# A planner that counts TensorE's instructions: 64-token recurrence blocks and an MLP on one core

## The chip, the core and the metric

The kernel runs on one core of a Trainium2 chip. Five engines share the core's SBUF: TensorE (matrix products, into PSUM), VectorE, ScalarE, GpSimd, and SyncE, which here only issues DMAs. The metric is device time in microseconds (us), median over several executions. One further execution was recorded by the hardware profiler; the page and the trace come from that one.

In the profile the engines are PE (TensorE's products), PEld (TensorE's weight loads, which overlap PE), DVE (VectorE), ACT (ScalarE), POOL (GpSimd) and SP (SyncE).

## What is computed

The first block is a linear recurrence (RWKV-6) over 768 tokens for 4 batches and 8 heads of 48 channels. Its output, with the heads side by side, is a row of 384 channels a token, which goes through a layer norm and a two-layer MLP with a residual.

```python
for t in range(S):
    kt, vt, rt, wt = (k[:, :, t], v[:, :, t], r[:, :, t], w[:, :, t])
    cur = np.einsum('bhd,bhe->bhde', u[None] * kt, vt)
    y[:, :, t] = np.einsum('bhd,bhde->bhe', rt, state + cur)
    state = wt[:, :, :, None] * state + np.einsum('bhd,bhe->bhde', kt, vt)
x = y.transpose(0, 2, 1, 3).reshape(B, S, H * D)
xn = (x - mean(x)) / np.sqrt(var(x) + 1e-06) * g_ln
out = x + np.maximum(xn @ w_ch1, 0.0) @ w_ch2        # 384 -> 1536 -> 384
```

## The kernel before

**Tiling.** The work is cut into 8 rounds: 4 batches by 2 halves of 384 tokens. A round has two units of 4 heads. Inside a round the recurrence is worked in blocks of 64 tokens by six levels of doubling. At level `lev`, `quads` multiplies `r` by `k` for the pairs of half blocks of that level, `keep` copies the wanted part of the result from PSUM into the matrix `A` (VectorE, under a mask), and `grow` multiplies `k` and then `r` in place by the decays of half a block (VectorE). So a round is a chain of quads, grow k, grow r, quads, and so on, six times over. Then `states` forms the sums that go from block to block, a scan on VectorE carries them, and `outputs` adds the parts up. `normalize`, `turn_x` and `mlp` follow; in the last three rounds the second layer of the MLP is done by `thirds`.

**Quarter products.** `quads`, `states` and `outputs` use a quarter of TensorE's array at a time, and four products in different quarters run beside each other. The planner calls them `tiled`. The products are very short. A float32 product takes two passes, and a pass is a weight load and a product, so a call of `quads` for both units is 192 instructions, `states` 96 a unit, and `outputs` up to 192 a unit. The other products (transposes, the MLP) use the whole array.

**Who sets the order.** No engine's order is written out by hand. Every step is handed to `Plan.add` (line 78) with its engine or engines, a planned cost in us, what it reads and writes, the tiles that it needs and a priority (40 times the round, plus a stage; the MLP's products are 200 later, so they fill). `Plan.order` (line 104) then plays the program forward: it keeps for each engine the time from which it is free, finds in `start_of` (line 123) when each ready step could start, and takes for the earliest engine the step with the smallest priority among those that could start within `WAIT` of the first. The steps are issued in the order of these planned starts, and each engine runs its own in that order, through the wrapper `InOrder` (line 32), whose calls all come from line 40. That is why nearly every row of the profile has line 40.

Constants of the planner (line 63): `HOP` 0.1 us from the end of a step to the start of one on another engine; `STAY` 12, a penalty on a change between quarter and whole products; `DRAIN` (line 64), 0.1 and 0.12 us for such a change.

**VectorE and GpSimd.** Small steps (`totals`, `own`, `own_term`, `halve`, `halve2`) may go to either. A step with `port=True`, and any that may go to GpSimd, is planned so that it doesn't run beside another such step on the other engine. On GpSimd it is planned beside a VectorE step without that mark, if there is one. In the program nothing holds it there: it starts as soon as its own inputs are ready.

**Filling.** In the first 90 planned us `idle` (line 1407) puts products of zeros into gaps over 0.4 us on TensorE.

Of the kernel before, what the change touches and what calls it, by code (L numbers as in the profile page):

```python
# [29 lines left out]


class InOrder:
    def __init__(self, tc, engine):
        self.tc, self.engine = tc, engine

    def __getattr__(self, name):
        f = getattr(self.engine, name)
        if not callable(f):
            return f
        return lambda *args, **kw: self.tc.keep_in_program_order(f(*args, **kw))  # L40


class Op:
    def __init__(self, i, costs, fn, pri, lat, size, port, tiled):
        self.i, self.costs, self.fn, self.pri = i, costs, fn, pri
        self.lat, self.size, self.port, self.tiled = lat, size, port, tiled
        self.need, self.next, self.new, self.uses = set(), [], [], set()
        self.ready, self.end, self.eng = 0.0, None, None


class Plan:
# [10 lines left out]

    HOP, PATIENCE, STAY = 0.1, 15.0, 12
    DRAIN = {True: 0.1, False: 0.12}
# [12 lines left out]

    def add(self, eng, cost, fn, r=(), w=(), new=(), pri=0, lat=0.0, size=0, port=False, tiled=False):
        costs = {eng: cost} if isinstance(eng, str) else dict(zip(eng, cost))
        op = Op(len(self.ops), costs, fn, pri, lat, size, port or "POOL" in costs, tiled)  # L80
        self.ops.append(op)
        for tag, name in new:
            self.tile_tag[name] = tag
            op.new.append((tag, name))
            self.queue[tag].append(op.i)
            self.maker[name] = op.i
        for key in list(r) + list(w):
            if key in self.writer:
                op.need.add(self.writer[key])
            name = key[0] if isinstance(key, tuple) else key  # L90
            op.uses.add(name)
        for tag, name in new:
            op.uses.add(name)
        for key in w:
            op.need.update(self.readers.pop(key, ()))
            self.writer[key] = op.i
        for key in r:
            self.readers.setdefault(key, set()).add(op.i)
        op.uses = {n for n in op.uses if n in self.tile_tag}
        op.need.update(self.maker.get(n, op.i) for n in op.uses)  # L100
        op.need.discard(op.i)
        return op

    def order(self, busy, idle=None, until=0.0):
        ops = self.ops
# [11 lines left out]
        for op in ops:  # L117
            if not left[op.i]:
                for e in op.costs:
                    ready[e].append(op)  # L120
        dma, todo, out, tiled = 0.0, len(ops), [], False

        def start_of(op, e):
# [15 lines left out]
            return t  # L139

        while todo:
            best = None
            for e, waiting in ready.items():
                at = [(t, op) for op in waiting if (t := start_of(op, e)) is not None]
                if not at:
                    continue
                first = min(t for t, _ in at)
                t, op = min(
                    ((t, op) for t, op in at if t <= first + self.WAIT[e]),
                    key=lambda x: (  # L150
                        x[1].pri + self.STAY * (e == "PE" and x[1].tiled != tiled), x[1].i
                    ),
                )
                if best is None or t < best[0]:
                    best = t, op, e
            assert best
            t, op, e = best
            if idle and e == "PE" and t < until and t - free["PE"] > 0.4 and self.homes[idle[0]]:
                n = int((t - free["PE"]) / (idle[1] * (2 if t < 5.0 else 1)))
                home = min(self.homes[idle[0]])  # L160
                if n and home[0] <= free["PE"]:
                    out.append((free["PE"], lambda n=n, home=home: idle[2](n, home[1])))
                    self.homes[idle[0]].remove(home)
                    self.homes[idle[0]].append((t, home[1]))
            if e == "PE" and op.tiled != tiled:
                tiled = op.tiled
                t += self.DRAIN[tiled]
            for x in op.costs:
                ready[x].remove(op)
            op.eng, op.start, cost = e, t, op.costs[e]  # L170
            free[e] = t + cost
# [16 lines left out]
            for j in op.next:  # L188
                nxt = ops[j]
                hop = self.HOP if set(nxt.costs) != {e} else 0.0  # L190
                nxt.ready = max(nxt.ready, op.end + hop)
                left[j] -= 1
                if not left[j]:
                    for x in nxt.costs:
                        ready[x].append(nxt)
            fn = op.fn
            out.append((t, fn if len(op.costs) == 1 else lambda fn=fn, e=e: fn(e)))
            todo -= 1
        return [fn for _, fn in out]


# [3 lines left out]
def kernel(  # L205
# [179 lines left out]
    def turn(nm, q, pr, stage):  # L385
# [20 lines left out]
        def keep(e="ACT"):  # L406
# [7 lines left out]
        plan.add(  # L414
            "PE", 0.66 if rows else 0.33, go, r=[key, (name, uu, pr)], w=[ps],
            new=[("b", ps)] + new, pri=at(rnd, stage), lat=0.17,
# [105 lines left out]
    def quads(rnd, lev, us=both_units):  # L522
        n, name = 1 << lev, f"a{rnd}_{lev}"

        def go():
# [21 lines left out]
            w=[(name, uu) for uu in us], new=[("a", name)] if us[0] == 0 else [],  # L547
            pri=at(rnd, 7 + 2 * lev), lat=0.17, tiled=True,
        )
# [82 lines left out]
    def turn_k(q, pr):  # L632
# [17 lines left out]
        key = (name, uu, pr)  # L650
        plan.add("PE", 0.33, go, r=[key], w=[ps], new=[("b", ps)], pri=at(rnd, 20), lat=0.17)
        plan.add("ACT", 0.45, back, r=[ps], w=[key], pri=at(rnd, 20) + EVICT / 2)
# [40 lines left out]
    def states(q):  # L693
# [19 lines left out]
        def scan():  # L713
# [19 lines left out]
            "PE", 0.55, go, r=parts_of(f"k{rnd}", [uu]) + [f"v{q}"], w=[kv_],  # L733
            new=[("a", kv_), ("s", s_)], pri=at(rnd, 22), lat=0.17, tiled=True,
        )
# [21 lines left out]
    def outputs(q, before):  # L757
# [4 lines left out]
        def go():  # L762
# [37 lines left out]
            w=[y_], new=[("a", y_)] + ([("x", x_)] if uu == 0 else []), pri=at(rnd, 24), lat=0.17,  # L800
            tiled=True,
        )
# [77 lines left out]
    def turn_x(rnd, kc):  # L880
# [15 lines left out]
        if rnd >= THREE:  # L896
# [4 lines left out]
        plan.add(  # L901
            "PE", 0.33, go, r=[f"xn{rnd}_{i}" for i in range(TT)], w=[ps], new=new,
            pri=pri, lat=0.17,
# [209 lines left out]
    def thirds(rnd, f):  # L1113
# [34 lines left out]
        for i in range(TT):  # L1148
# [42 lines left out]
            if first:  # L1191
                need += [(f"x{NR - 1}", uu, j) for uu in both_units for j in range(2)]
            plan.add(
                "PE", 0.525, both, r=need, w=keys,
                new=[("a" if i < 2 else "b", n) for n in names] if first else [],
# [7 lines left out]
    def mlp(rnd):  # L1203
# [3 lines left out]
        for f in range(FC):  # L1207
# [3 lines left out]
            if rnd < THREE:  # L1211
# [8 lines left out]
                def relu(f=f, ps=ps, h_=h_):  # L1220
                    ACT.activation(out=tile_("h", h_, [P, RN]), in_=tiles[ps], func=AF.Relu)

                plan.add(
                    "PE", 1.95, go,
                    r=[(f"w1_{g}", kc) for kc in range(KC)] + [f"xf{rnd}_{kc}" for kc in range(KC)],
# [38 lines left out]
            def relu(h_=h_):  # L1264
                ACT.activation(out=tiles[h_], in_=tiles[h_], func=AF.Relu)

            plan.add(
                "PE", 0.53, go_d, r=[d_] + [x_keys(rnd, kc)[2] for kc in range(KC)], w=[ps_d, ps_d + "t"],
                new=[("b", ps_d), (tag, h_)], pri=pri,
# [3 lines left out]
            plan.add(  # L1273
                "PE", 1.12, go,
                r=[(f"wl{g}", kc) for kc in range(KC)] + [(f"wh{g}", kc) for kc in range(KC)]
# [11 lines left out]
        for i in range(TT):  # L1287
            o = f"o{rnd}_{i}"
            for f in range(0, FC, KC):
                def go(f=f, i=i, o=o):  # L1290
# [8 lines left out]
                plan.add(  # L1299
                    "PE", 1.95, go,  # L1300
                    r=[f"h{rnd}_{f_}" for f_ in range(f, f + KC)] + [f"ffn2_{f_}" for f_ in range(f, f + KC)],
# [147 lines left out]
```

## Time and profile before

The times of three executions are 549.24 (the median), 553.76 and 548.67 us. The profiled execution took 550.61 us, of which its span, from the first to the last instruction, is 548.9 us.

| what | us | note |
|---|---|---|
| span of the profiled execution | 548.9 | 20355 instructions |
| the profiled execution itself | 550.61 | 1.7 us around the span |
| mean granted clock of TensorE | 0.993 | as a share of full speed |
| the chain's share of TensorE | 76% | of VectorE 14%, DMA 4%, "issue" 3% |
| quads' products (`a<-r,k`) | 70.0 busy | 4608 passes, 212 ns each, overlapping |
| MLP, second layer (`o<-ffn,h`) | 123.7 busy | 360 passes |
| grow on k and r (`k<-k,tot`, `r<-r,tot`) | 44.4 and 44.0 busy | 45 each, on VectorE |
| GpSimd in all | 84.7 busy | 111 instructions |

"Busy" is the time in which an engine had an instruction of that group under way. The chain is followed back from the last instruction, at each step to what released it; its shares say where time would have to go for the end to move. "issue" means that the engine waited for nothing that the profile shows.

### The profile page before, as it was taken

Reading aid. Unit: us, or ns where it says so; the run is one execution under the profiler, and the core shown is the slowest. Engines: PE = TensorE matmul, PEld = TensorE weight load, DVE = VectorE, ACT = ScalarE, POOL = GpSimd, SP = SyncE. Lnnn points to the kernel's source line nnn. Section 1 sums busy time; section 2 is a strip of 40 time slices with the busy share of each in tenths; the row PEclk is TensorE's granted clock in tenths of the full one; section 3 lists DMA queues with packets and bytes.
Section 4 is the critical chain, followed back from the end, with each engine's and each line's share of the span. In section 5 each row is a group of like instructions: output and inputs, shape, how many; then the busy total and the mean of one; then the engine's idle time right before and its main releaser. Section 6 shows DMA issues by size and latency. Waiting matters only on the chain.

```text
span 548.9 us, 20355 instructions
## 1 busy us (share of the span) xinstructions
PE 523.8 (95%) x8928; PEld 429.5 (78%) x8928; DVE 409.5 (75%) x806; ACT 266.4 (49%) x579; POOL 84.7 (15%) x111
## 2 busy tenths in 40 slices
PE   8999999999999989899999999999999999999995
PEld 7776676666887667688876789758866999999994
DVE  5797999878988969889897697714854856756554
ACT  4787987642654442364640683605830433333321
POOL 7032004701212152103410020000300000000000
PEclk9998999999999999999999999999999999999999
DMA  9974854457453627437540244104201311312201
GB/s 276 260 197 99 247 135 74 99 139 197 121 113 59 165 45 139 85 82 145 120 102 22 54 107 103 36 16 110 68 16 43 116 59 59 100 59 86 73 2 43
DMA packets 118840, 55.83 MB, mean 102 GB/s; under 512 B 86880, under 2 KB 115680, under 8 KB 118752
## 3 DMA queue, kind: packets, MB, share of 16 engines
q1 hardware_dynamic: 117168, 53.65, 38.9%
q8 instruction: 70, 1.15, 0.9%
q10 hardware_dynamic: 1584, 0.88, 0.6%
q14 instruction: 18, 0.15, 0.1%
HBM read 45.05 MB, written 7.10 MB: 95 GB/s over the span
## 4 chain that ended last, share of the span: by engine, by line
PE 76%; DVE 14%; DMA 4%; issue 3%; SPq 2%; ACT 1%; POOL 0%; DVEq 0%; POOLq 0%; ACTq 0%
PE a L40 21%; PE o L40 17%; PE h_ps L40 17%; PE hd_ps L40 7%; DVE k L40 3%; DVE r L40 3%; PE w_ps L40 2%; PE idle L40 2%; PE k_ps L40 2%; PE o_2P L40 2%; SPq L40 2%; PE kn_ps L40 2%; DVE x L40 1%; PE xT_ps L40 1%; PE r_ps L40 1%
## 5 line engine op out<-in xcount | busy, mean ns | idle before, releaser
L40 PE MATMUL o<-ffn,h 128*128 128x384 f32 x360 | 123.7, 489 | 0.0
L40 PEld LDWEIGHTS o<-ffn,h 128*128 128x128 f32 x360 | 65.7, 190 | 37.9
L40 PEld LDWEIGHTS a<-r,k 48*63 48x63 f32 (+5 forms) x4608 | 63.8, 126 | 27.5 <-DVE r L40 11.1
L40 PE MATMUL a<-r,k 48*63 48x32 f32 (+5 forms) x4608 | 70.0, 212 | 10.3 <-DVE r L40 5.4
L40 ACT COPY h<-hd_ps 128x384 f32<-128x384 f32 x84 | 40.0, 479 | 74.5 <-PE hd_ps L40 72.9
L40 DVE SCALAR_TENSOR_TENSOR h<-h_ps,h 128x384 f32<-128x384 f32 x84 | 46.2, 553 | 34.2 <-PE h_ps L40 33.4
L40 PE MATMUL h_ps<-xhl,wl 128*128 128x384 f32 x252 | 61.0, 350 | 0.3
L40 PE MATMUL h_ps<-xhl,wh 128*128 128x384 f32 x252 | 58.0, 338 | 0.0
L40 PE MATMUL hd_ps<-xd,d 128*128 128x384 f32 x252 | 56.8, 351 | 0.6 <-DVE h L40 0.5
L40 DVE TENSOR_TENSOR k<-k,tot 112x768 f32<-112x768 f32 (+1 forms) x45 | 44.4, 987 | 14.1 <-PE a L40 13.9
L40 PEld LDWEIGHTS h_ps<-xhl,wl 128*128 128x128 f32 x252 | 43.7, 188 | 3.5 <-ACT h L40 1.1
L40 PEld LDWEIGHTS hd_ps<-xd,d 128*128 128x128 f32 x252 | 44.1, 190 | 2.2 <-DVE h L40 1.2
L40 PEld LDWEIGHTS h_ps<-xhl,wh 128*128 128x128 f32 x252 | 45.5, 188 | 0.0
L40 DVE TENSOR_TENSOR r<-r,tot 112x768 f32<-112x768 f32 (+1 forms) x45 | 44.0, 977 | 0.0
L40 DVE COPY_PREDICATED A<-mask,a 128x768 f32<-128x768 int8 x32 | 38.5, 1203 | 3.5 <-PE a L40 3.5
L40 POOL TENSOR_TENSOR rk<-nat,nat 128x576 f32<-128x576 f32 x11 | 18.5, 1680 | 143.1 <-DVE own L40 68.0
L40 ACT ACTIVATE hH<-h 128x384 fp32r<-128x384 f32 x36 | 18.8, 525 | 41.1 <-DVE h L40 41.1
L40 ACT ACTIVATE h<-h 128x384 f32<-128x384 f32 x48 | 25.1, 526 | 27.9 <-DVE h L40 27.6
L40 DVE SCALAR_TENSOR_TENSOR hL<-h,hH 128x384 fp32r<-128x384 f32 x36 | 20.0, 555 | 14.3 <-ACT hH L40 14.1
L40 ACT COPY A<-a 32x384 f32<-32x384 f32 x32 | 14.9, 467 | 30.0 <-PE a L40 27.4
L40 ACT COPY w<-w_ps 112x384 f32<-112x384 f32 x32 | 14.4, 482 | 27.5 <-PE w_ps L40 26.9
L40 PE MATMUL a<-w2d,hD 128*128 128x384 f32 x72 | 25.4, 353 | 0.8 <-DVE hD L40 0.7
(118 smaller groups left out, 1020.6 us busy)
## 6 DMA issues: line engine op xcount, KB each, us to landing
d<-w1d SPq DMA_DIRECT2D x84, 192.0 KB, 2.7
raw<-in_moe_w_ch_dram SPq DMA_DIRECT2D x24, 384.0 KB, 4.0
v<-in_v_dram SPq DMA_DIRECT2D x48, 96.0 KB, 3.2
out_dram<-x SPq DMA_DIRECT2D x24, 192.0 KB, 2.0
nat<-in_w_dram SPq DMA_DIRECT2D x36, 96.0 KB, 3.0
nat<-in_k_dram SPq DMA_DIRECT2D x36, 96.0 KB, 2.9
nat<-in_r_dram SPq DMA_DIRECT2D x36, 96.0 KB, 2.8
vx<-v SPq DMA_DIRECT2D x32, 72.0 KB, 2.9
```

Source lines behind the costliest of these rows:

```text
L40: return lambda *args, **kw: self.tc.keep_in_program_order(f(*args, **kw))
```

## The change

1. Every TensorE step gets a `count`, the number of its instructions: 6 for three transposes of one pass, 12 where there are two passes, 96 for each unit of `quads` and `states`, 192 (176 in the first round) for `outputs`. `order` keeps a running `count`, starting at 50, and the time `ahead` at which the next piece of 256 instructions is there. `fetches` goes over the borders between pieces that a step would cross: it adds the wait until that piece is there, and sets the next one 4.3 us later. The wait is added to the step's planned cost.
2. When a step is chosen on TensorE, a step that would wait for a piece by more than 0.2 us gets 300 added to its priority (`switching`), which puts it behind the fillers.
3. From 60 planned us on, a quarter product counts as ready 0.3 us after what it needs has ended, where it was 0.1 us.
4. A `port` step on GpSimd gets extra dependencies. If the VectorE step planned last (`beside`) is still running in the plan, the GpSimd step waits in the program for what that step needs and for the VectorE step before it (`before`); if it isn't, it waits for `beside` itself. What the GpSimd step needs anyway, and steps of GpSimd, are left out. `InOrder` adds these to the first instruction of the step as data dependencies.

```diff
 class InOrder:
+    waits, last = [], None
...
-        return lambda *args, **kw: self.tc.keep_in_program_order(f(*args, **kw))
+        def call(*args, **kw):
+            ins = self.tc.keep_in_program_order(f(*args, **kw))
+            for other in InOrder.waits:
+                self.tc.add_manual_dep(ins.ins, other.name, AFTER, reason="port")
+            InOrder.waits, InOrder.last = [], ins.ins
+            return ins
...
-    HOP, PATIENCE, STAY = 0.1, 15.0, 12
+    HOP, MARGIN, FILLED, PATIENCE, STAY = 0.1, 0.3, 60.0, 15.0, 12
+    BEFORE, PIECE, FETCH, CROWD = 50, 256, 4.3, 300
...
+        count, ahead = self.BEFORE, 0.0
+        beside = before = None
...
+        def fetches(t, op):
+            waits, after = 0.0, ahead
+            for at in range(-count % self.PIECE, op.count, self.PIECE):
+                now = t + waits + op.costs["PE"] * at / op.count
+                waits += max(after - now, 0.0)
+                after = max(now, after) + self.FETCH
+            return waits, after
+
+        def switching(t, op):
+            drain = self.DRAIN[op.tiled] * (op.tiled != tiled)
+            waits = fetches(t + drain, op)[0] > 2 * self.DRAIN[True]
+            return self.STAY * (op.tiled != tiled) + self.CROWD * waits
...
-                    key=lambda x: (
-                        x[1].pri + self.STAY * (e == "PE" and x[1].tiled != tiled), x[1].i
-                    ),
+                    key=lambda x: (x[1].pri + (switching(*x) if e == "PE" else 0), x[1].i),
...
+                    count += 4 * -(-n // 3)
...
+            fetched = 0.0
+            if e == "PE":
+                fetched, ahead = fetches(t, op)
+                count += op.count
...
-            op.eng, op.start, cost = e, t, op.costs[e]
+            op.eng, op.start, cost = e, t, op.costs[e] + fetched
...
-                hop = self.HOP if set(nxt.costs) != {e} else 0.0
+                hop = 0.0 if set(nxt.costs) == {e} else self.HOP
+                if nxt.tiled and self.FILLED < op.end:
+                    hop = self.MARGIN
...
+            if e == "DVE":
+                beside, before = op, beside
+            if e == "POOL" and op.port:
+                others = set(beside.need) if beside and beside.end > t + 0.05 else set()
+                others |= {x.i for x in (before if others else beside,) if x}
+                others -= op.need
+                others = [ops[i] for i in sorted(others) if ops[i].eng not in (None, "POOL")]
+            else:
+                others = ()
+            out.append((t, lambda fn=fn, op=op, others=others: self.run(fn, op, others)))
...
-            "PE", 0.7 * len(us) * (C - n + 6) / (C + 6), go,
...
-            pri=at(rnd, 7 + 2 * lev), lat=0.17, tiled=True,
+            pri=at(rnd, 7 + 2 * lev), lat=0.17, tiled=True, count=96 * len(us),
```

## The prediction

> **What bounds the kernel now.** I read the page's busy row and chain first, then the waits of TensorE, its timeline at those waits, the fetch queue, and a table of windows.
>
> ```profile
> PE 523.8 (95%) x8928; PEld 429.5 (78%) x8928; DVE 409.5 (75%) x806; ACT 266.4 (49%) x579; POOL 84.7 (15%) x111
> ...
> q8 instruction: 70, 1.15, 0.9%
> ...
> PE 76%; DVE 14%; DMA 4%; issue 3%; SPq 2%; ACT 1%; POOL 0%; DVEq 0%; POOLq 0%; ACTq 0%
> ```
>
> TensorE is busy in all but 25.1 us of 548.9, and the chain runs through it. Its work doesn't change, so only idle time, fillers and a lower clock can be won. The waits of TensorE (us in total, times, longest):
>
> ```profile
> PE a L40 <- issue: 8.0, 7, 1.5
> PE a L40 <- DVE r L40: 5.4, 7, 1.2
> ```
>
> Timeline rows of such a wait, idle time and releaser in brackets:
>
> ```profile
> 226.58 2.30 PE L40 MATMUL a<-r,k 48*32 48x32 f32 x175
> 230.42 0.43 PE L40 MATMUL a<-r,k 48*63 48x32 f32 x17 [1.54 <-issue]
> ```
>
> 192 passes of two levels of quads, back to back, stop after 175 for a reason that no semaphore explains. Counting TensorE's records in order (weight loads, products, and waits that are instructions of their own), the seven "issue" stalls come before records 705, 1985, 4289, 5057, 6593, 8385 and 9665: each 193 more than a multiple of 256. Queue 8 carried 70 packets, 1.15 MB, 16 KB or 256 instructions each. The stalled records follow the landing of the last packet by 1.25 to 1.56 us. So TensorE waits for instructions: **8.0 us**.
>
> The clock, in the windows (the figure after POOL's count is the granted clock):
>
> ```profile
> 228.00:230.00 2.00, 0.88 (x63) 0.77 (x56) 1.90 (x3) 1.52 (x4) 0.00 (x0) 1.00 0.31 107
> ...
> 232.00:234.00 2.00, 2.00 (x10) 1.64 (x8) 0.00 (x0) 1.32 (x3) 0.49 (x2) 0.50 0.00 0
> ```
>
> It is at a half in two spells of 3.4 us, at 46.6 and 230.9 us, right after the 1.27 and 1.54 us stalls: 1.7 us lost in each.
>
> The rest of the idle time, from gaps over 0.4 us: eleven gaps between 35 and 393 us that end on VectorE or ScalarE, 0.57 + 0.84 + 0.43 + 0.46 + 0.83 + 1.23 + 0.86 + 0.77 + 0.78 + 0.74 + 0.50 = **8.0 us**; the start, 1.2; the last sums and stores, 4.6. The start and end stay.
>
> [...]
>
> ```profile
> L40 DVE TENSOR_TENSOR r<-r,tot x45: 544/951/2170, 18.9 to 350.2; 112x768 f32<-112x768 f32 x35, 112x384 f32<-112x384 f32 x10
> ...
> L40 DVE TENSOR_TENSOR vo<-v,own x7: 743/759/2391, 44.3 to 319.6; 128x576 f32<-128x576 f32 x7
> ```
>
> (minimum, median, longest in ns.) [...]
>
> **Part 1: counting and holding back.** Quads for both units, 192 instructions, take about 1.40 us (the chain's pieces of 96 passes: mostly 1.2 to 1.6), so 256 of them run in 1.87 us. A piece needs some 3.0 us: the next fetch mostly began 0.7 to 1.6 us after a border, the packet takes 0.9, and the first instruction follows 1.3 later. I laid the built kernels' instruction orders out in pieces from record 193, and priced a piece's passes at 0.0146 us for quads and outputs (1.40/96), 0.0115 for states, 0.324 for `o` (1.94/6), 0.176 for `hd_ps` and its like (1.06/6), 0.11 for transposes (1.33/12), and the planner's 0.11 for a change of kind. Pieces under 3.2 us:
> - before, nine: 2.71, 2.36, 2.99, 1.87, 2.84, 1.87, 1.87, 2.46, 2.26. Five of them stalled (1.27, 1.14, 0.75, 1.04, 1.54); the other two stalls (1.19, 1.06) followed a fetch that began over 3 us late.
> - after, eight: 2.71, 3.06, 1.87, 1.87, 1.87, 2.43, 2.08, 1.87.
>
> So short pieces do **not** go away. The reason is in the count: it leaves out the waits that are instructions of their own (116 in the trace) and starts at 50, where the trace has the first border at 193, so 63. Laid out by the planner's own count the changed order has only four pieces under 3.3 us; by the record the borders come 13 to some 100 instructions earlier. Price after: five pieces near 1.87 to 2.08 at 1.0 (of such pieces before: 1.14, 1.04, 1.54, and 2.26 with none; mean 0.93) is 5.0, and 0.7 for the rest: 5.7. Saved **2.3 us**; ends 0 and 6.
>
> **Part 2: the margin, and the order that follows.** What TensorE has to do between the end of one level's quads and the next level's, against grow k and grow r (0.95 each) and two hops: before, 8 of the 35 such places in rounds 1 to 7 have under 3.0 us (2.16 to 2.91); after, 4 (2.22 to 2.91), and the median goes from about 4 to 7 us. Gaps of 8.0 us halve: **4.0 us** saved; ends 0 and 7. What this costs: the later levels come up to 9 us of TensorE work later, and the MLP behind them is lacking as cover later on. The end isn't exposed: from 400 us TensorE is dense, and the pieces of the built orders from the 64th on hold the same work within 2%.
>
> **Part 3: fillers.** Five passes fewer, two products of 384 and one of 256: 2 x 0.65 + 0.43 = 1.7 us. They stand in idle time; I take half, **0.9**; ends 0 and 1.7.
>
> **Part 4: the ties.** 61 operations of GpSimd on two inputs are left of 75; 53 of them wait for VectorE (26 before) and 42 for TensorE (4 before), that is for the quarter product that the VectorE step beside them needs. Behind a waiting one stand GpSimd's later steps; what waits for those is VectorE's `own` sums, `grow` (by `tot`), the scans (by `decay`) and `x<-a,vo`. Before, no wait of VectorE ends on GpSimd, and GpSimd has 0% of the chain, so a small delay is free. Moved to VectorE, by the built orders: `tot` and `decay` 2 x 0.95 + 2 x 0.56 + 4 x 0.36 + 2 x 0.26 + 2 x 0.21 + 0.18 = 5.6; `rk` 4 x 0.75 = 3.0; `vo` 2 x 0.76 = 1.5; `w1diff` less `w1rest` 0; five `w2t` back to GpSimd, -2.8: **+7.3 us of VectorE**, most of it between 60 and 340 us, where it is busy 84% (201.64 of 240 from 100 to 340). Against it stands stretching[...]: grow k 35 x (1.111 - 0.951) = 5.6, grow r 5.3 with the short form, `vo` 2.8, `w2t` 1.6, `w1diff` 1.2: 16.5 us, of which the ties may take half. VectorE's 14% of the chain against 75% busy puts about a fifth of either on the path: -1.6 and +1.4. Net 0; ends -3 and +6, since a consumer on VectorE held by GpSimd is not shown before.
>
> **Part 5: the clock.** Two spells, 1.7 us each. The first piece pair (1.87, 1.87, near 50 us) is no better than before; I leave both. Ends -3.4 and +3.4.
>
> Sum: -2.3 - 4.0 - 0.9 + 0 = -7.2 us. Against the profiled execution's 550.6 (548.9 and 1.7 around it) that is 543.4. It stands 1.4 above the median of 549.24, so in terms of the median **542 us**.
>
> **Rivals.**
> - *Nothing moves.* The miscounted borders only place the stalls elsewhere (8.0 again), and what the margin saves is lost where cover is missing later. For it: eight short pieces against nine. Against it: fewer places with thin cover. 549, within 3.
> - *GpSimd comes late* (slower). The 42 operations that now wait for a quarter product start with their neighbour on VectorE and end 1.2 to 1.7 us (`vo`, `rk` on GpSimd) later; if every third holds an in-order VectorE step by one grow's length, 14 x 0.95 = 13 us, and the gain elsewhere is 4, the time is 558. It decides from when VectorE's waits for GpSimd pass some 7 us and TensorE's gaps before `a` grow with them. For it: VectorE is full in places (19.65 of 20 from 140 to 160 us). Against it: VectorE idles 139 us, and GpSimd has fewer chains of `tot`.
> - *The count works after all*: 8.0 us of stalls, one spell of low clock (1.7) and 5 of the gaps go: 534. For it: by its own count the order is nearly clean, and a fetch that begins early covers a piece of 2.3. Against it: the layout above.
>
> **How the numbers follow.** A measurement of this kernel can tell about 1% (5.5 us) from no change. Forecast (up to 546, the full count with 0.12 among it) 0.54; nothing moves (546 to 552) 0.28; GpSimd late (over 552) 0.18. Of the first some 0.50 lies below 543.7 (1% under 549.24) and 0.04 above; of the last 0.02 lies under 554.7. So faster 0.50, within 1% 0.34, slower 0.16. The range of 8 in 10 leaves out 0.06 below 534 (half of the full count's) and 0.14 above 554 (0.04 of the last case is under it): 534 to 554.
>
> **What would show it.** Right: "issue" before `a` on TensorE at 5 to 6 us, still at records 193 past a multiple of 256; gaps that end on `r` of VectorE halved; the longest grow under 1.5 us; no wait of VectorE on GpSimd over 3 us. Wrong: "issue" near 0 (the count holds) or over 8; VectorE waiting for GpSimd; new gaps before 400 us that end on VectorE's `own`, `tot` or `x`; more spells at half clock.

## The result, and the profile after

The change moved the time by almost nothing. Over 20 executions each, the changed kernel takes 548.79 us (median; 545.65 to 555.92) and the kernel before, beside it on the same chip, 550.55. The ratio is **0.9978, with a 95% interval of 0.9957 to 0.9999**: 0.2% faster, where 542 us and a clear gain had been forecast.

The profiled execution took 552.50 us (span 550.8), 3.7 above its own median; that of before, 550.61, lies at the median of its twenty (550.55). Ratios leave disturbed executions out and medians don't, so the two needn't agree, and sizes below come from the ratios; of the run *tr* only two of 13 executions were left, and not the profiled one, so its ratio is shown and not used.

Four lines of the page of the changed kernel: busy time, granted clock by fortieths of the span, the fetch queue, the chain.

```profile
PE 526.4 (96%) x8922; PEld 431.7 (78%) x8922; DVE 403.8 (73%) x820; ACT 266.1 (48%) x579; POOL 66.4 (12%) x97
...
PEclk9988999999999999979999999999999999999999
...
q8 instruction: 70, 1.15, 0.9%
...
PE 83%; DVE 7%; DMA 3%; ACT 3%; issue 2%; SPq 1%; DVEq 0%; ACTq 0%
```

VectorE's share of the chain has halved, from 14% to 7%. TensorE has 2.6 us more of busy time for six passes fewer, and the clock row suggests why: it dips in the third and fourth slice and in the 18th. The spells at half clock are 3.4 us at 36.2, 6.8 at 49.8 and 6.8 at 237.6, where before had 3.4 at 46.6 and 3.4 at 230.9. The mean clock of this execution is 0.982 (0.993 before).

TensorE's waits (us in total, times, longest):

```profile
PE a L49 <- issue: 7.4, 8, 1.8
PE kn_ps L49 <- DVE k L49: 2.1, 1, 2.1
...
PE h_ps L49 <- issue: 1.0, 1, 1.0
...
PE a L49 <- DVE r L49: 0.9, 1, 0.9
...
PE hd_ps L49 <- issue: 0.5, 1, 0.5
```

The three "issue" rows make 8.9 us in ten stalls (8.0 in seven before). Each of the ten still stands at a record 193 past a multiple of 256: 961, 1217, 1473, 1985, 2241, 4545, 5313, 7105, 8641 and 13761. The longest in the timeline:

```profile
211.27 1.41 PE L49 MATMUL a<-r,k 48*60 48x32 f32 x89
214.47 0.31 PE L49 MATMUL a<-r,k 48*60 48x32 f32 x7 [1.79 <-issue]
```

Quads stop after 89 of their 96 passes, and the last 7 come 1.79 us later with no semaphore between them. A short piece isn't the only way to such a stall. Four of the ten (records 1985, 4545, 7105 and 8641, 5.2 us) end a piece that TensorE got through in 1.8 to 2.6 us. Five (961, 1217, 1473, 2241 and 13761, 3.2 us) end a piece that lasted 4.2 to 5.9 us; there the packet with the next piece began only 3.0 to 5.1 us after the border before. The tenth (5313, 0.5 us) had a packet that took 1.9 us. Four of those five lie before 54 us; why fetches begin so late there no run shows.

The rest of the idle time did shrink: gaps over 0.25 us between 30 and 420 us that aren't at a border fell from 8.0 us (11) to 6.2 (7). The row of grow r (duration in ns: least, median, longest):

```profile
L49 DVE TENSOR_TENSOR r<-r,tot x45: 545/951/958, 18.7 to 362.8; 112x768 f32<-112x768 f32 x35, 112x384 f32<-112x384 f32 x10
```

The median is as before; the longest is 958 where it was 2170. No grow r is stretched any more. Whether the ties or the new order did that, *no_ties* below tells.

So the things that the change was to improve went different ways: VectorE's part did improve, the fetch stalls didn't, and the clock got worse. That asks which part did which.

### The profile page after: what moved, and what is told of

It is laid out like the page before. It is cut to its first block, busy times and chain, and to the rows that moved or that the text cites. A ratio compares the mean times of both kernels' runs of the same rounds, so it can differ in the third digit from the quotient of the medians.

```text
span 550.8 us, 20398 instructions
## 1 busy us (share of the span) xinstructions
PE 526.4 (96%) x8922; PEld 431.7 (78%) x8922; DVE 403.8 (73%) x820; ACT 266.1 (48%) x579; POOL 66.4 (12%) x97
## 4 chain that ended last, share of the span: by engine, by line
PE 83%; DVE 7%; DMA 3%; ACT 3%; issue 2%; SPq 1%; DVEq 0%; ACTq 0%
PE a L49 23%; PE o L49 21%; PE h_ps L49 19%; PE hd_ps L49 7%; PE r_ps L49 3%; PE w_ps L49 2%; PE k_ps L49 2%; PE o_2P L49 2%; PE kn_ps L49 2%; DVE x L49 2%; PE xT_ps L49 1%; DMA raw<-in_moe_w_ch_dram 1%; PE idle L49 1%; PE o_2D L49 1%; ACT held L49 1%
## 5 line engine op out<-in xcount | busy, mean ns | idle before, releaser
L49 PEld LDWEIGHTS a<-r,k 48*32 48x32 f32 (+5 forms) x4608 | 64.3, 127 | 22.7 <-issue 12.3
L49 DVE SCALAR_TENSOR_TENSOR h<-h_ps,h 128x384 f32<-128x384 f32 x84 | 46.6, 556 | 44.7 <-PE h_ps L49 42.9
L49 PE MATMUL a<-r,k 48*32 48x32 f32 (+5 forms) x4608 | 70.2, 213 | 7.0 <-issue 5.9
L49 DVE TENSOR_TENSOR k<-k,tot 112x768 f32<-112x768 f32 (+1 forms) x45 | 39.3, 872 | 22.3 <-PE a L49 21.9
L49 DVE TENSOR_TENSOR r<-r,tot 112x768 f32<-112x768 f32 (+1 forms) x45 | 38.8, 863 | 0.0
L49 PEld LDWEIGHTS a<-v,A 64*64 64x64 f32 x384 | 22.1, 138 | 5.2 <-issue 3.6
```

The costliest lines, as they stand in the source:

```text
L49: ins = self.tc.keep_in_program_order(f(*args, **kw))
```

## The experiments

"Border" is the idle time of TensorE in stops over 0.25 us at records 193 past a multiple of 256, "other" that of its other gaps over 0.25 us that end between 30 and 420 us, both from the one profiled execution, in us; "clock" is the mean granted clock over all executions of that kernel.

| run | what it has | ratio to before, 95% | median us | clock | border | other |
|---|---|---|---|---|---|---|
| (before) | | | 550.5 | 0.993 | 8.0 | 8.0 |
| (the change) | ties, margin, count | 0.9978 [0.9957, 0.9999] | 548.8 | 0.985 | 8.9 | 6.2 |
| same | nothing | 0.9985 [0.9958, 1.0011] | 550.2 | 0.992 | 7.0 | 8.1 |
| ties_only | ties | 0.9861 [0.9823, 0.9899] | 543.6 | 0.992 | 8.4 | 1.7 |
| margin_only | margin | 0.9932 [0.9894, 0.9971] | 549.7 | 0.992 | 10.5 | 4.3 |
| count_only | count | 1.0026 [1.0003, 1.0048] | 551.7 | 0.986 | 9.0 | 6.8 |
| no_ties | margin, count | 1.0018 [0.9990, 1.0046] | 552.0 | 0.984 | 10.4 | 7.2 |
| no_count | ties, margin | 0.9875 [0.9844, 0.9907] | 545.9 | 0.993 | 10.3 | 1.4 |
| exact | all, right count | 1.0006 [0.9979, 1.0033] | 552.0 | 0.987 | 5.6 | 9.0 |
| exact_no_ties | margin, right count | 1.0073 [1.0046, 1.0101] | 556.3 | 0.987 | 3.3 | 10.9 |
| thin_idle | ties, narrow fillers | 0.9991 [0.9968, 1.0014] | 548.6 | 0.971 | 7.7 | 6.4 |
| late_count | all, count from 60 us | 1.0039 [1.0013, 1.0066] | 551.4 | 0.987 | 11.2 | 5.0 |
| late_exact | all, right count from 60 us | 0.9911 [0.9878, 0.9945] | 543.5 | 0.994 | 1.9 | 7.0 |
| late_exact_nm | ties, right count from 60 us | **0.9841 [0.9815, 0.9868]** | 539.7 | 0.997 | 1.9 | 5.3 |
| tc | ties, count | 0.9980 [0.9957, 1.0002] | 549.4 | 0.987 | 11.0 | 3.5 |
| tr | ties, right count | (0.9908) | 553.3 | 0.985 | 4.5 | 10.6 |
| tc_late | ties, count from 60 us | 0.9914 [0.9880, 0.9948] | 546.0 | 0.991 | 8.3 | 1.5 |
| tr_half | ties, count half a piece off, from 60 us | 0.9976 [0.9953, 1.0000] | 549.9 | 0.989 | 11.1 | 0.8 |

The readings to be told apart: the ties and the margin win and the count loses it again, since its borders lie where no border is; or the ties take away what the margin wins; or no part moves anything.

### One part alone

*same* is the kernel before once more, for the size of the noise.

> The kernel before, unchanged. It is here for the spread of its granted clock, which the profile shows for one execution only (0.993, two half-clock spells of 3.4 us). Clock theory (the changed kernel's gaps shrank, but it spends longer at half clock: 17.1 us against 6.8 in the profiles): this kernel's executions have a mean clock of 0.990 or more, the changed kernel's twenty had 0.985, and 0.005 x 550 = 2.7 us of the gain went there. Rival (the clock is the same on average and the two profiles only happened to differ): mean clock 0.984 to 0.987 here too.

*ties_only*, against the changed kernel:

```diff
-            return self.STAY * (op.tiled != tiled) + self.CROWD * waits
+            return self.STAY * (op.tiled != tiled)
...
-                fetched, ahead = fetches(t, op)
-                count += op.count
+                pass
...
-                if nxt.tiled and self.FILLED < op.end:
+                if False:
```

> The kernel before with the extra dependencies of GpSimd alone: every engine's order is that of the kernel before. The changed kernel without the ties had 1.0018, with them 0.9978, at the same clock (0.984 and 0.985). Theory A (the ties gain 2 us, and the half-clock time comes with the order alone): mean clock 0.992 to 0.994, the same as before; time at full clock (time less span times 1 less the clock) 544 to 546, against 546.9 before; ratio 0.995 to 0.998. Theory B (ties only help an order that has slack on GpSimd): within 0.2% of before. Theory C (GpSimd late): VectorE waits 3 us or more on GpSimd, ratio over 1.003.

*margin_only* leaves the third of these lines as the change has it, and adds no dependencies. *count_only* keeps the count and its penalty, and leaves out the margin and the dependencies:

```diff
-                if nxt.tiled and self.FILLED < op.end:
+                if False:
...
-            if e == "POOL" and op.port:
+            if False:
```

> The kernel before with the margin of 0.3 us alone. Laid out by the record its short pieces lack 8.5 us (6.7 before). Theory A (what lengthens the half-clock time is the count, which lays stalls and long gaps among quarter products): mean clock 0.990 to 0.994, time at full clock 544 to 546, ratio 0.995 to 0.999. Theory B (any new order does; the clock follows from where long gaps happen to fall): mean clock 0.984 to 0.988, ratio 1.000 to 1.004.

> The kernel before with the count and the penalty alone; no margin, no ties. Laid out by the record its short pieces lack 6.7 us, as before. Count theory: idle time at borders 7 to 10 us, no less than before (8.0), and 548 to 553 us. Rival (the count as written already does part of its work, and the margin spoiled it): idle time at borders under 5 us and 543 to 547 us.

The ties alone are worth 1.4%, some six times what the whole change brings, and more than any theory in the run's expectation. Their order on the engines is that of before, and so is the number of instructions. From the page and from the tile row of grow r:

```profile
PE 522.5 (97%) x8928; PEld 429.2 (79%) x8928; DVE 396.8 (73%) x806; ACT 266.7 (49%) x579; POOL 77.4 (14%) x111
```

```profile
L49 DVE TENSOR_TENSOR r<-r,tot x45: 548/951/955, 18.8 to 343.5; 112x768 f32<-112x768 f32 x35, 112x384 f32<-112x384 f32 x10
```

806 and 111 instructions, as before, but VectorE is busy 396.8 us instead of 409.5 and GpSimd 77.4 instead of 84.7: the same operations, each in less time. `vo` on VectorE took 1163 ns on average before and 766 here. And the gaps outside the borders fall from 8.0 to 1.7 us. So nearly all of them had come from a grow (or a step before one) that ran longer beside a GpSimd operation.

The margin alone nearly halves the gaps (8.0 to 4.3) and wins 0.7%. The count alone loses 0.3%, at a lower clock and with no less time at the borders. The three sum to -1.8%; the change as a whole has -0.2%.

### One part left out

*no_ties* and *no_count* are the changed kernel with one of the edits above.

> The changed kernel without the extra dependencies of GpSimd; every engine's order is the same. Theory that the ties gain (VectorE's grow is no longer stretched[...]: mean 0.87 us against 0.99): grow's mean goes back to about 0.98, VectorE's busy time from 404 up to 412 to 420 us, gaps on TensorE that end on VectorE grow by 1 to 4 us, and 550 to 553 us. Theory that they cost (GpSimd's results come late): 544 to 547. Theory that they do nothing for the end: within 1 us of the changed kernel.

> The changed kernel without the count: margin and ties, the order of margin_only. Theory A: clock 0.990 to 0.994, time at full clock 542 to 544 (margin and ties add up), 545 to 548 us, ratio 0.990 to 0.995, the best so far. Theory B: clock 0.984 to 0.988, ratio 0.997 to 1.001, no better than the changed kernel.

In the changed kernel the ties are worth less: 0.4%, or 2.2 us (1.0018 and 0.9978; 0.3 to 4.1 with both intervals). VectorE is busy 411.4 us without them and 403.8 with them, but not because of grow r. Its row in *no_ties*:

```profile
L49 DVE TENSOR_TENSOR r<-r,tot x45: 545/948/976, 19.8 to 362.0; 112x768 f32<-112x768 f32 x35, 112x384 f32<-112x384 f32 x10
```

In the order of the change grow r isn't stretched even without the ties, against what the run's expectation said. So what the ties are worth depends on the order that they are added to.

Ties and margin together win 1.25%, no more than the ties alone: they remove the same gaps (1.4 us are left, 1.7 without the margin). Adding the count to these two takes the ratio from 0.9875 to 0.9978: **5.7 us lost** (0.0103 of 550.5; 3.6 to 7.8 with both intervals). The border time falls a little (10.3 to 8.9), the other gaps rise from 1.4 to 6.2, and the mean clock falls from 0.993 to 0.985. The same loss shows beside the ties alone (*ties_only* and *tc*, 0.9861 and 0.9980) and beside the margin alone (*margin_only* and *no_ties*, 0.9932 and 1.0018): wherever the count is added, it takes away most or all of what the rest had won.

In these profiles most of it goes in the first stage. Windows of 17 to 75 us, of the changed kernel and then of no_count (busy us and instructions of PE, PEld, DVE, ACT and POOL, then the granted clock, the share of DMA, GB/s):

```profile
17.00:75.00 58.00, 52.19 (x1016) 38.90 (x1013) 45.95 (x112) 46.18 (x99) 13.71 (x29) 0.91 0.73 200
```

```profile
17.00:75.00 58.00, 54.63 (x1212) 40.45 (x1205) 49.57 (x115) 48.46 (x103) 13.08 (x29) 1.00 0.72 201
```

With the count 1016 passes fall in these 58 us, without it 1212; that alone proves little, since another order has other passes there. But TensorE has 2.4 us more of idle time there and loses 9% of the clock, 5.2 us of 58. These 7.6 us are more than the 6.5 by which the two spans differ; later each has 6.8 us at half clock. In the profiles of all seven kernels that plan the count from the start, right or as written, TensorE is idle for 4.3 to 7.6 us of this window; in the others it is 1.9 to 3.8, but for thin_idle (5.6). The clock in this window isn't low in all of the seven: two of them (*no_ties* and *exact*) had 1.00 in the profiled execution.

### The clock

What makes TensorE drop to half clock? In the traces of the kernel before and of the change, the spells before 540 us last 3.41 or 6.83 us, and within a trace they start whole multiples of 3.41 us apart (in the kernel before 184.3 us, 54 of them). Each began within 1.3 us after a stop of TensorE: four after a stall among quarter products (1.27 and 1.54 us before; 1.16 and 0.80 with the change), the fifth after a wait of 2.07 us for grow k. But the length of a stop alone doesn't decide: no spell came within 20 us after the stalls of 1.65 and 1.79 us that end at 119.9 and 214.5 us in the changed kernel. From the trace I summed for each window of 3.41 us, in step with the spells, the columns of all passes, each times the share of the array that it uses. In the kernel before, windows with 763 and 1076 preceded the two spells, and 1317 and 1485 did not; in the changed kernel 789, 824, 981, 1070 and 1092 did, and 1209 did not (981 and 1092 lie in a spell, and prolong it). The fullest window of before has 7680. Quads alone, back to back at full clock, run at a pace of 1170 to 1400 a window, by level. So, as an estimate from these sums, quads keep the clock with little to spare, and a stall of about 1.2 us among them can lose it. The sum is no sharp bound. Over the 17 traces that have a spell between 8 and 532 us, 32 of the 36 spells begin after a window of 1162 or less, the other four after 1312, 1348, 1395 and 2422; and four windows of 996 to 1042 at full clock were not followed by one.

That is an observation. *thin_idle* tests it: ties_only with the same passes in the same order, but the fillers' zeros 8 columns wide in place of 128 to 384. Nothing in the output depends on them.

```diff
-                t[:, 0 : now * P], zeros, nought.broadcast_to([P, now * P]), start=True, stop=True
+                t[:, 0:8], zeros, nought.broadcast_to([P, 8]), start=True, stop=True
```

> The kernel with the ties alone (ratio 0.986, mean clock 0.992), in the same order and with the same instructions, but each product of zeros that fills TensorE's gaps in the first 60 us has 8 columns in place of 128 to 384: the array does next to nothing in those gaps. No result depends on them. Clock theory[...]: more spells before 60 us, mean clock down by 0.006 to 0.018 (one to three spells of 3.4 us), time at full clock within 1 us of 539.8, so 545 to 553 us and ratio 0.99 to 1.00. Rival (half clock is only a sign, TensorE waits there anyway): the clock falls and the time doesn't, ratio 0.984 to 0.988. Second rival (the clock doesn't follow what the array does): clock 0.990 to 0.994.

It took 548.6 us against 543.6 (ratios 0.9991 and 0.9861), at a mean clock of 0.971 against 0.992: work that nobody uses is worth 5 us by the medians and 7 by the ratios. One window of each, 17 to 28 us, thin_idle first and then ties_only:

```profile
17.00:28.00 11.00, 10.74 (x176) 9.73 (x177) 7.94 (x12) 5.33 (x11) 4.08 (x15) 0.53 1.02 297
```

```profile
17.00:28.00 11.00, 9.92 (x265) 8.31 (x261) 8.53 (x13) 7.47 (x16) 4.14 (x15) 1.00 1.01 280
```

thin_idle is the busier of the two, 98% of the window, at half the clock, and gets through 176 passes where the other does 265. So being busier (98% against 90%) did not keep TensorE's clock up here. Two parts of the expectation missed. The clock fell by 0.021, a little more than was expected, and the time at full clock (time less span times 1 less the clock) wasn't within 1 us of 539.8 but 532.6. So time wasn't lost here in proportion to the clock; that some of the half-clock spells fell where TensorE would have waited or filled anyway is likely, and not shown.

How much of the 5.7 us is clock? Three prices are at hand for 0.01 of mean clock. The 75 executions of before that were run beside *same*, *exact*, *no_ties* and *count_only* differ among themselves, and there it goes with 4.2 us. A whole span per unit of clock would be 5.5. In thin_idle, the one run that moves the clock by itself, 0.021 cost 5 to 7 us, so it is 2.4 to 3.4. The change from 0.9932 to 0.9848 is then worth 2.0 to 4.6 us, by estimate: **a third to four fifths of what the count costs**. The rest would be idle time.

### The right count

Is the count bad because it is wrong? *exact* starts it at 70 and adds 0.57% for the waits that are instructions of their own, so that the planned borders lie where the trace has them:

```diff
-    BEFORE, PIECE, FETCH, CROWD = 50, 256, 4.3, 300
+    BEFORE, PIECE, FETCH, CROWD = 70, 256, 4.3, 300
...
-            for at in range(-count % self.PIECE, op.count, self.PIECE):
+            for at in range(int(-count % self.PIECE), op.count, self.PIECE):
...
-                count += op.count
+                count += op.count * 1.0057
```

> The changed kernel with the planner's count put right: it starts at 70, not 50, and adds 0.57% for the waits that are instructions of their own, so that its borders fall where the record has them. Laid out by the record, pieces under 3.1 us lack 0.7 us in all, against 7.1 in the changed kernel and 6.7 before. Count theory (the stalls stayed because the borders were miscounted): idle time before records 193 past a multiple of 256 falls from 8.9 us to under 3; half-clock spells, which follow stalls among quarter products, fall from 17.1 us to at most 7; 541 to 545 us, 1.0 to 1.7% faster than before. Rival (the stalls come from fetches that begin late, wherever the border is): 6 us or more of such idle time remains, and the time stays within 0.5% of the changed kernel's 548.8. Second rival (steps held back cost as much in gaps on VectorE as the stalls did): stalls under 3 us but gaps that end on VectorE grow from 5.6 to 9 us or more, and 547 to 550 us.

*exact_no_ties* is the same without the dependencies.

> The kernel with the corrected count, without the ties, in the same order. With the ties (exact) TensorE stood still for 4.8 us at 262.8, behind a chain from a late transfer of r over GpSimd's rk and VectorE's rk to grow, and the time was 1.0006 of before. Theory A (that stop is the ties' doing, since they set GpSimd's step later): the stop is under 1.5 us, time at full clock 541 to 543, ratio 0.995 to 0.999. Theory B (the order itself has the late transfer in it): a stop of 4 us or more at the same place, time at full clock 546 to 548 (2 us for the ties on top of 544.9), ratio 1.003 to 1.006.

The borders did get better (5.6 and 3.3 us), and the time did not: 1.0006 and 1.0073. Of the 5.6 us, 3.5 still fall before 60 us; two of these stalls, at records 705 and 961, followed packets that began 4.3 and 5.1 us after the border before, so right borders don't prevent them. In *exact* one stop is 4.8 us long. Its timeline row, and the chain that led to it (start, us, what):

```profile
267.58 1.38 PE L49 MATMUL a<-r,k 48*32 48x32 f32 x96 [4.81 <-DVE r L49]
```

```profile
258.85 3.95 DMA nat<-in_r_dram
...
263.14 1.41 POOL rk L49
...
265.25 0.95 DVE k L49
```

A load of `r` that lands at 262.8 us holds `rk` on GpSimd, behind which VectorE's own `rk`, grow k and grow r and then the quads wait. The load is issued only at 258.8 us. I took this for the ties' doing. But *exact_no_ties* has the same stop at the same record without them (4.72 us), and *tr*, without the margin, has one of 5.88 us behind the same chain: all three kernels that plan the right count from the start have it, so it belongs to their order. The ties are worth 0.7% here too (1.0073 and 1.0006).

### The count from 60 us on

If the first stage is what the count spoils, it must be worth something later. *late_count* is the change with

```diff
             waits, after = 0.0, ahead
+            if t < self.FILLED:
+                return waits, after
```

*late_exact* has this and the right count; *late_exact_nm* has no margin besides.

> The changed kernel (margin, ties, count as written) with the waits for instructions planned only from 60 us on; before that it goes in the order of the kernel before, with 19 products of zeros as there, not 16. Margin and ties alone: 0.9875, clock 0.993; with the count from the start: 0.9978, clock 0.985. Theory E (the count does its harm in the first 60 us: counted waits leave fewer gaps for zeros[...]): clock 0.990 to 0.994, ratio 0.986 to 0.990. Theory L (it does it later, by long gaps among quarter products): clock 0.984 to 0.987, ratio 0.995 to 0.999.

> The same with the count put right (70 at the start, 0.57% added). Laid out by the record its short pieces lack 2.5 us, against 6.5 with the count as written and 8.5 without one. If holding quarter products back at the true borders helps: idle time at borders after 60 us under 3.5 us, time at full clock 537 to 540, and with a clock of 0.990 to 0.994 a ratio of 0.978 to 0.984. Rival (what is held back comes late for VectorE, and the gaps return): idle at borders under 3.5 us but gaps that end on VectorE 5 us or more (1.4 without the count), time at full clock 541 to 544, ratio 0.987 or more.

> As late_exact, without the margin of 0.3 us: ties and the corrected count after 60 us. Ties alone: 0.9861, gaps on VectorE 1.7 us, at borders 8.4 us. If the true borders help: borders under 4 us, time at full clock 535 to 539, ratio 0.975 to 0.983. Rival: what is saved at borders comes back as gaps on VectorE or on transfers; ratio 0.985 to 0.990.

With the count as written nothing is won: 11.2 us at the borders, and 1.0039, slower than the change itself. With the right count the stalls after 60 us go from 5.5 (before) to 0.55 and to 0, and the clock stays up. *late_exact_nm*, its clock row on the page and the first rows of TensorE's waits:

```profile
PEclk9999999999999999999999999999999999999999
```

```profile
PE a L49 <- issue: 1.9, 3, 0.9
PE k_ps L49 <- DMA nat<-in_k_dram: 1.3, 2, 0.8
PE hd_ps L49 <- DVE h L49: 1.3, 1, 1.3
PE a L49 <- DVE r L49: 1.1, 1, 1.1
```

There is no spell at half clock before the end. At 539.7 us it beats both kernels. But what the borders gave (8.4 to 1.9 against ties_only) was in good part paid in other gaps (1.7 to 5.3), where TensorE now waits for VectorE and for loads. Its interval, from six executions, overlaps that of the ties alone, so whether a right count adds to them is not settled. With the margin it adds nothing: *late_exact* has 0.9911 and no_count 0.9875, as the rival in its expectation said.

### Wrong place or wrong time?

Two explanations of the count's loss stood: it is misplaced, or its planning of the first 60 us is harmful. Four kernels with the ties and no margin set them apart: the count as written (*tc*) and right (*tr*) from the start, as written from 60 us (*tc_late*), and the right one from 60 us shifted by half a piece:

```diff
-    BEFORE, PIECE, FETCH, CROWD = 70, 256, 4.3, 300
+    BEFORE, PIECE, FETCH, CROWD = 198, 256, 4.3, 300
```

> The changed kernel without the margin: ties, and the count as written from the start (the order of count_only, which had 1.0026 at a clock of 0.986). Theory M (misplaced borders): idle time at borders 8 to 10 us, clock 0.985 to 0.988, ratio 0.992 to 0.998. Theory E (the first 60 us): the same here; the other three tell.

> Ties and the right count from the start, no margin. Theory M: borders after 60 us under 3 us, ratio 0.982 to 0.988, like late_exact_nm. Theory E: clock 0.985 to 0.988 with spells before 60 us, ratio 0.993 or more.

> Ties and the count as written, from 60 us on, no margin; it differs from late_exact_nm (0.9841) only in where the borders are placed (20 to 100 instructions late). Theory M: borders after 60 us 5 to 9 us, clock 0.986 to 0.990, ratio 0.992 to 1.002. Theory E: ratio 0.984 to 0.989.

> late_exact_nm with its borders 128 instructions off, half a piece. Laid out by the record its short pieces lack 9.0 us, against 2.5. Theory M: borders after 60 us 6 to 10 us, ratio 0.992 to 1.004. Rival (any order with fewer quarter products in a row gains): borders under 4 us, ratio 0.984 to 0.988.

The place is shown to matter. From 60 us on, the ratio is 0.9841 with the borders right, 0.9914 as written, and 0.9976 half a piece off, with 0, 5.6 and 8.9 us of stalls after 60 us: a wrong count costs 0.7 to 1.4% against a right one. (The first ran on another chip than the other two, each beside the kernel before.) Against the ties alone (0.9861), of these three only the one half a piece off is clearly slower.

For the early start the runs disagree. Without the margin, the count as written costs 0.7% more when it starts at once than from 60 us on (0.9980 and 0.9914). With the margin it is the other way about: 0.9978 at once and 1.0039 from 60 us on. For the right count *tr* gives no usable ratio; with the margin starting at once costs 0.95%, or 5.2 us, more (1.0006 and 0.9911), but *exact* has its stop of 4.8 us at 267 us, far from the first stage. So an early count leaves TensorE idle for longer in the first stage in every profile, and what is left of that at the end depends on the rest of the order. Nor is the low clock bound to the early stage: *late_count*, with no count before 60 us, has 0.987 and the most time at the borders.

## Why the prediction was wrong

**What bounds the kernel**: right, idle time and clock of TensorE. Between the two profiles the clock moved more: the time at half clock before the end went from 6.8 to 17.1 us, the idle time at borders and elsewhere from 16.0 to 15.1.

**Part 1, "Saved 2.3 us; ends 0 and 6": the step that failed.** Its layout held in the main. By the record, not by the planner's count, short pieces remain, and six of the eight that were named stalled, for 0.43 + 0.80 + 0.74 + 1.65 + 0.98 + 1.79 = 6.4 us where 5.7 were priced. Four other borders added 2.5, so 8.9 in all: nothing saved. It took the next fetch to begin 0.7 to 1.6 us after a border; at five of the ten stalls, two of the six among them, it began 3.0 to 5.1 us after. The larger error is the end at 0. If the borders are misplaced, then "nothing gained" isn't the worst, since the planned waits still change the order. In place of 2.3 us saved, the count costs 5.7 us beside the other two parts (3.6 to 7.8), and 1.4 alone: gaps outside the borders rise from 1.4 to 6.2 us, and the mean clock falls from 0.993 to 0.985.

**Part 2, "Gaps of 8.0 us halve: 4.0 us saved"**: right for the margin alone (8.0 to 4.3 us of gaps, 3.7 us of time, 1.6 to 5.8 by its interval). In the change the gaps fell to 6.2 only, and the margin adds nothing to the ties, which remove the same gaps (0.9978 with it, 0.9980 in *tc* without): summing Parts 2 and 4 as if they were separate was an error that their sizes hid.

**Part 3, "Fillers", 0.9**: six passes went, the two of each of three products, not five, and nothing was won that the runs show. They were taken for idle time that costs something; thin_idle shows that they hold the clock up (a mean of 0.992 with them at full width, 0.971 at 8 columns).

**Part 4, "Net 0; ends -3 and +6": right within its ends for the change, mis-sized for the ties.** In the order of the change the ties are worth 2.2 us (0.3 to 4.1). Alone, in the order of before, they are worth 7.7 (5.6 to 9.7), outside the range. The stretch of 16.5 us was read rightly from the rows, but VectorE's busy time fell by 12.7, not by half of it. And "about a fifth of either on the path" took VectorE's average share for operations that stand in the chain quads, grow k, grow r, quads. Of the 12.7 us, 7.7 came off the time, three fifths, and 6.3 us of gaps vanished. That GpSimd's operations beside VectorE's do the stretching, the traces show: in the kernel before, each of the five grow r over 1 us (1751 to 2170 ns) runs beside `rk`, `vo` or `w1rest` on GpSimd, and the ties alone, in the same order, leave a longest grow r of 955 ns. By what mechanism isn't shown.

**Part 5, "I leave both"**: wrong. The mean clock fell from 0.993 to 0.985. The prediction named more spells at half clock as a sign that it was wrong, and its end of 3.4 us is inside the 2.0 to 4.6 that the clock is estimated to have cost.

Set against the runs, ties and margin were forecast at 4.0 us and brought 6.9; count, fillers and clock were forecast at 3.2 and cost 5.7. The two errors have opposite signs, and the second is the larger. A smaller one: the last step took 1.4 us off, since the profiled execution stood that far above a median of three; over twenty it stands at the median, so the sum said 543.4, not 542.

**The rivals.** "Nothing moves" has the right number, 549, by luck, and half of the mechanism: the miscounted borders do only place the stalls elsewhere. But the margin's gain isn't lost for want of cover; 6.9 us gained and 5.7 lost cancel. "GpSimd comes late" didn't happen: VectorE's longest wait for GpSimd in the changed kernel is 1.2 us. "The count works after all" fell for the change; a right count after 60 us does end the stalls there.

**Open.** How the count's order lowers the clock no run separates: fewer fillers (34 passes against 40), quads left alone, or both. Fewer fillers aren't the whole of it, since *exact* has 50 and a mean clock of 0.987. Why the instruction fetches of the first stage begin late is open too, and so is why the order of the right count holds the load of `r` until 258.8 us.

## What to carry to other kernels

A planner that models a resource must be checked against the trace's own count of it: borders half a piece off cost 1.4% (7.4 us) against right ones, about what all the stalls that they were to prevent had cost. A stretched operation should be priced by the chain it stands in, not by its engine's average share of the path; here the ties alone brought 7.7 us, where the whole change brought 1.2. And where small products use little of the array (quads, back to back, 1170 to 1400 weighted columns a window, of 7680 in the fullest), look at the granted clock by stage before taking out idle filling: with the narrow filling it was 0.53 here from 17 to 28 us, in place of 1.00.

## What the hardware showed unexpectedly

- TensorE at 98% busy ran at 0.53 of its clock for 11 us (thin_idle). What went with half clock is how much of the array the passes use: 32 of 36 spells began after a window of at most 1162 weighted columns, of 7680 in the fullest, but a few windows on either side break the rule.
- The stalls at instruction pieces come at the same records modulo 256 in every order tried, and in the changed kernel all ten end 1.28 to 1.51 us after the packet's landing. In the first 55 us of that kernel packets mostly began 2.1 to 5.1 us after a border, where later the prediction's 0.7 to 1.6 us is common.
- Products of zeros were worth 5 to 7 us of 549, in an order otherwise the same.
